# Gated attention and gMLP kernel: the first product of each group is moved to a second PSUM bank by ScalarE and the second product is accumulated onto it there

## The chip, the cores and the metric

The kernel runs on one core of one Trainium2 chip. The metric is the device time of one execution in microseconds (us), from the first to the last instruction of the program with what lies around it. The kernel before took 688.05 us, the median of three runs (686.73, 688.05 and 689.18 us).

## The reference

One input `x` (2048 rows of 1024) goes through two branches, and a gate per row mixes them:

```
gate = sigmoid(sum(x * gate_w))                       # one number per row
# branch A: 32 heads of 32, each row attends to 8 rows at distances 0, 2, ... 14
q, k, v = split(x @ wqkv)
a = softmax(q . k[i - 2w] / sqrt(32)) . v[i - 2w]     # w = 0..7, masked before row 0
a = a @ wo
# branch B: gMLP with F = 3584, Fh = 1792
z  = gelu(x @ w_in);  z1 = z[:, :Fh];  z2 = layernorm(z[:, Fh:])
g  = w_sp @ z2 + b_sp                                 # w_sp is 2048 x 2048: it mixes rows
b  = (z1 * g) @ w_out
out = gate * a + (1 - gate) * b
```

All inputs are bfloat16, and so is the output (2048 by 1024).

## The kernel before, in words

Rows are cut into 16 tiles of 128, which lie in the partitions. TensorE works through five stages, one after the other, in an order that is written out by hand:

1. Projections. `qkv_tile` (matmuls on L603) makes q, k and v for one of eight groups of four heads and one row tile, `z2_tile` (L308) makes z2 in slices of 448 columns. ScalarE copies each finished PSUM bank out (L611, L314). q, k and v are stored to DRAM and come back in a layout in which VectorE can do the sliding attention alone.
2. The z1 stage (L706): 64 tiles of eight matmuls of 448 columns. ScalarE takes each out through a GELU (L708) into one of two staging buffers, which SyncE's queue stores to `z1_d` after every fourth tile (L713). Beside it ScalarE takes sums of squares of z2 (`squares`, L667) and of absolute values of `w_out` (`w_norm`, L539); the latter's pieces are loaded by `load_w_piece` (L536) into two slots by turns. `row_store` (L461 to L470) puts two small transposes into a PSUM bank (L463, L464), which VectorE reads (L465, L466), and stores row scales to DRAM (L470).
3. Mixing, w_sp by z2, 16 groups (`g_group`). A group is a pair of row tiles by half of the columns. A two by two block product is made with seven block products in place of eight (Winograd's scheme of sums); each block product is eight matmuls of 448 columns (L719, the helper `product`). VectorE makes the sums of the operands (L481 to L490). Three banks hold the partial results: `pa` goes on accumulating while ScalarE copies intermediate states of it out (`keep`, L729 and L731, into a ring of five buffers `snaps`), `pd` likewise, and `pb` holds one product alone. VectorE adds a state and a bank, or two states (`vec`, L735), which gives three of the four blocks of g; ScalarE writes the fourth (L762). VectorE then multiplies by z1 (L763). `y_norm` (L559, ScalarE) and `y_scale` (L573, VectorE) rescale the result, and `store_y` (L529) writes it to DRAM from a ring of four buffers, which the groups write by turns.
4. The attention's output by wo (L869), taken out by ScalarE with the gate as scale (L871) into `mix`. It reads `wo` (L439, 2048 KB) and the transposed attention result (L444, 16 transposing DMAs).
5. The last stage, y by w_out, eight groups of seven block products of 512 columns, seven matmuls each (L719 again). `hold` (L880) copies states out with a scale, VectorE adds `mix` to them (L898, L904, L907), and `finish` (L884) scales a bank, adds, and rounds.

The attention itself (L331 to L371) is some 50 VectorE instructions for each group of heads, the longest 4.4 us. It runs beside stages 1 to 3.

The order on each engine is that in which the Python program emits instructions; there is no later scheduler. `Beat` sets it: `beat.now` is a clock that counts TensorE's columns, `beat.vector` one that counts the time that VectorE will be taken for. Each helper of a stage advances the first (`beat.run`) or the second (`beat.on_vector`). Work that is not tied to a matmul waits in a heap with a due time (`beat.at`), and the attention's steps come from a generator, each with a time that it takes. `flush` emits an attention step once its start, by the two clocks, is no more than `LEAD` (3.0 us) ahead of `beat.now`; it stands in VectorE's queue from there on, ahead of whatever the stage emits next. All DMAs of this kernel are issued from SyncE's one queue, in the emitted order; an issue that waits holds back all behind it.

[...] One pool of eight (`psum`, tag "ps") serves all tiles of all stages, so a tile waits until the reader of an earlier tile in the same bank is done.

Of the kernel before, what the change touches and what calls it, by code (L numbers as in the profile page):

```python
# [10 lines left out]
F32 = mybir.dt.float32  # L11
# [4 lines left out]
P = 128  # L16
# [13 lines left out]
ZC = 448  # L30
# [4 lines left out]
W2P = FH + 32  # L35
BEAT = 1.0 / 2360.0
LEAD = 3.0
NU = S // 256
FL = FH // 2
L1_EARLY = 10  # L40
# [20 lines left out]
def kernel(  # L61
# [13 lines left out]
    nc = tc.nc  # L75
# [2 lines left out]

    apool = ctx.enter_context(tc.tile_pool(name="arena", bufs=1))
    sm = ctx.enter_context(tc.tile_pool(name="small", bufs=1))  # L80
    psum = ctx.enter_context(tc.tile_pool(name="psum", bufs=8, space=bass.MemoryType.PSUM))
    dpool = ctx.enter_context(tc.tile_pool(name="dscratch", bufs=1, space=bass.MemoryType.DRAM))

    arena = apool.tile([P, ARENA], BF, name="arena")
# [1 line left out]
    def reg(off, n):  # L86
        return arena[:, off:off + n]
# [10 lines left out]
    warm = reg(R_OFF + 35200, 512)  # L98
    nc.vector.memset(warm, 0.0)

    def warm_up(n):
        pw = psum.tile([P, 512], F32, name="pw", tag="ps")
        for _ in range(n):
            nc.tensor.matmul(pw[:], warm[:, 0:P], warm, start=True, stop=True)

    ident = sm.tile([P, P], BF, name="ident")
    make_identity(nc, ident[:])
# [3 lines left out]
    for jh in range(2):  # L111
        for w in range(W):
            n = min(8, max(0, 14 - 2 * w - 8 * jh))
# [60 lines left out]
    b21, b22 = z2h[:, 8:16, 0:FL], z2h[:, 8:16, FL:FH]  # L174
    t1, t2, t4 = [reg(o, 8 * FL).bitcast(F16).rearrange("p (k f) -> p k f", k=8) for o in (T1_OFF, T2_OFF, T4_OFF)]
# [27 lines left out]
    d11, d12, d21, d22 = [wv[:, h, :, 512 * c:512 * (c + 1)] for h in range(2) for c in range(2)]  # L203
    e1, e2, e4 = [reg(F_OFF + 3584 * r, 3584).bitcast(F16).rearrange("p (k n) -> p k n", n=512) for r in range(3)]
# [29 lines left out]
    class Beat:  # L234
        def __init__(self):
            self.now = 0.0
            self.n = 0
            self.later = []
            self.vector = 0.0
            self.steps = None  # L240
            self.step = None

        def at(self, t, fn):
            heapq.heappush(self.later, (t, self.n, fn))
# [9 lines left out]
        def flush(self, t):  # L254
            while True:
                if self.steps is not None and self.step is None:
                    self.step = next(self.steps, None)
                    if self.step is None:
                        self.steps = None
                due = self.later[0][0] if self.later else 1e12  # L260
                start = max(self.step[0], self.vector) if self.step else 1e12
                if min(due, start - LEAD) > t:
                    return
                if due <= start - LEAD:
                    heapq.heappop(self.later)[2]()
                else:
                    self.vector = start + self.step[1]
                    fn, self.step = self.step[2], None
                    fn()

    beat = Beat()
# [53 lines left out]
    TT = nc.vector.tensor_tensor  # L325
# [209 lines left out]
    def load_w_piece(m):  # L535
        sync.dma_start(w_pieces[m % 2], w_flat[:, 1792 * m:1792 * (m + 1)])  # L536
# [97 lines left out]
    for n in range(L1_EARLY):  # L634
        t = beat.now + 8.0 + 13.0 * n
# [19 lines left out]
    t = beat.now  # L655
# [17 lines left out]
    for i in range(16):  # L673
        for c in range(1 if i > 1 else 2, 4):
            z2_tile(i, c)
        n = L1_EARLY + (i - 3) // 2
# [7 lines left out]
    t = beat.now  # L684
# [3 lines left out]
    beat.at(t + 20.0, row_store)  # L688
    beat.at(t + 22.0, lambda: load_scale(0))
    for m in range(8):  # L690
        beat.at(t + 32.0 + 4.2 * m, lambda m=m: load_w_piece(m))
        beat.at(t + 36.5 + 4.2 * m, lambda m=m: w_norm(m))
    beat.at(t + 70.0, w_total)
    beat.at(t + 91.0, w_power)
# [1 line left out]
    for c in range(4):  # L696
# [3 lines left out]
        for i in range(16):  # L700
# [3 lines left out]
            ps = psum.tile([P, 512], F32, name="ps", tag="ps")  # L704
            for kt in range(KT):
                nc.tensor.matmul(ps[:, 0:ZC], xT[:, kt, i * P:(i + 1) * P], w1[:, kt, :],  # L706
                                 start=(kt == 0), stop=(kt == KT - 1))
# [4 lines left out]
            if i % 4 == 3:  # L712
                sync.dma_start(bass.AP(tensor=z1_d.tensor, offset=z1_d.offset + (i - 3) * P * FH + (2 * (c % 2) + c // 2) * ZC,  # L713
                                       ap=[[FH, P], [P * FH, 4], [1, ZC]]), z1s)
    assert prep["done"]
    def product(ps, w, v, c0, c1, first):
        K = v.shape[1]
        for k in range(K):
            nc.tensor.matmul(ps[:, 0:c1 - c0], w[:, k, :], v[:, k, c0:c1], start=(first and k == 0),  # L719
                             stop=(k == K - 1), skip_group_check=True)  # L720
        beat.run(K * (c1 - c0))
# [3 lines left out]
    def keep(ps, bias):  # L725
        out = snaps[snap[0] % 5]
        snap[0] += 1
        if bias is None:
            nc.scalar.copy(out, ps[:, 0:ZC])  # L729
        else:  # L730
            nc.scalar.activation(out, ps[:, 0:ZC], ACT.Identity, bias=bias)  # L731
        return out

    def vec(out, a, b):
        TT(out, a, b, ALU.add)  # L735
        beat.on_vector(0.65)

    def g_group(n):
        u, f0 = n // 2, n % 2 * ZC
        f1 = f0 + ZC  # L740
        v = pairs[u % 2]
        lo, hi = [bt[:, 2 * u + h:2 * u + h + 1] for h in range(2)]
        g, z = g_ring[n % 4], z1_ring[n % 2]
        now(("z1", n), ("y", u - 2))
        pa, pb, pd = [psum.tile([P, 512], F32, name="ps", tag="ps") for _ in range(3)]
        product(pa, v.a11, b11, f0, f1, True)
        p1 = keep(pa, lo)
        product(pb, v.a12, b21, f0, f1, True)
        vec(g[:, 0, 0], pb[:, 0:ZC], p1)
        product(pa, v.s2, t2, f0, f1, False)  # L750
        u2 = keep(pa, lo)
        product(pd, v.s1, t1, f0, f1, True)
        p5 = keep(pd, None)
        product(pa, v.s3, t3, f0, f1, False)
        u3 = keep(pa, hi)
        if n > 0:
            y_norm(n - 1)
        vec(g[:, 1, 1], p5, u3)
        product(pd, v.s4, b22, f0, f1, False)
        vec(g[:, 0, 1], pd[:, 0:ZC], u2)  # L760
        product(pa, v.a22, t4, f0, f1, False)
        nc.scalar.activation(g[:, 1, 0], pa[:, 0:ZC], ACT.Identity, bias=hi)  # L762
        TT(g, g, z, ALU.mult)  # L763
        beat.on_vector(1.1)
        if n + 2 < 2 * NU:
            soon(("z1", n + 2), lambda: load_z1(n + 2))
# [16 lines left out]
    def y_finish(u):  # L783
        def scaled():
            y_power(u)
            y_scale(u)
            soon(("y", u), lambda: y_done(u))
            if u == NU - 1:
                beat.at(max(beat.now, beat.vector) + 0.6, lambda: load_w_out(1))
# [3 lines left out]
    for n in range(2):  # L793
        load_z1(n)
    for n in range(2 * NU):
        u, fb = n // 2, n % 2
        t = beat.now
        if fb == 0 and u + 1 < NU:
            beat.at(t + 0.5, lambda u=u: load_scale(u + 1))
# [3 lines left out]
        if fb == 0 and u > 0:  # L803
            y_finish(u - 1)
        if fb == 0 and u + 1 < NU:
            for h in range(2):
# [5 lines left out]
        if prep["attended"]:  # L812
            limit = 16 if n >= 2 * NU - 3 else 11
            for m in range(6):
# [3 lines left out]
    t = beat.now  # L818
# [44 lines left out]
    for a in range(16):  # L863
        if a == 12:
            beat.at(beat.now + 0.5, lambda: load_rows_y(2))
        for c in range(2):
            psa = psum.tile([P, 512], F32, name="psa", tag="ps")
            for kt in range(KT):
                nc.tensor.matmul(psa[:], oT[a][:, kt, :], wo_sb[:, kt, 512 * c:512 * (c + 1)],  # L869
                                 start=(kt == 0), stop=(kt == KT - 1))  # L870
# [6 lines left out]
    def hold(ps, scale):  # L877
        out = keeps[kept[0] % 7]
        kept[0] += 1
        nc.scalar.activation(out, ps[:], ACT.Copy, scale=scale)  # L880
        return out

    def finish(out, ps, scale, x):
        nc.vector.scalar_tensor_tensor(out, ps[:], scale, x, ALU.mult, ALU.add)  # L884

    for u in range(NU):
        v = rows[u % 5]
        lo, hi = [omr[:, 2 * u + h:2 * u + h + 1] for h in range(2)]
        m11, m12, m21, m22 = [mix[2 * u + h][:, 512 * c:512 * (c + 1)] for h in range(2) for c in range(2)]
        o11, o12, o21, o22 = [ob_slots[2 * u + h][:, 512 * c:512 * (c + 1)] for h in range(2) for c in range(2)]  # L890
        pa, pb, pd = [psum.tile([P, 512], F32, name="ps", tag="ps") for _ in range(3)]
        if u == 0:
            for n in (3, 4):
                load_rows_y(n)
        product(pa, v.a11, d11, 0, 512, True)
        p1 = hold(pa, lo)
        product(pb, v.a12, d21, 0, 512, True)
        TT(p1, p1, m11, ALU.add)  # L898
        finish(o11, pb, lo, p1)
        product(pa, v.s2, e2, 0, 512, False)  # L900
        u2 = hold(pa, lo)
        product(pd, v.s1, e1, 0, 512, True)
        p5 = hold(pd, hi)
        TT(u2, u2, m12, ALU.add)  # L904
        product(pa, v.s3, e3, 0, 512, False)
        u3 = hold(pa, hi)
        TT(p5, p5, m22, ALU.add)  # L907
        if 0 < u < NU - 1:
            y_sums(u + 1)
        product(pd, v.s4, d22, 0, 512, False)  # L910
        TT(o22, p5, u3, ALU.add)
        finish(o12, pd, lo, u2)
        sync.dma_start(out2[2 * u * P:(2 * u + 1) * P, :], ob_slots[2 * u])
        product(pa, v.a22, e4, 0, 512, False)
        finish(o21, pa, hi, m21)
        if u == NU - 1:
            sync.dma_start(out2[(2 * u + 1) * P:(2 * u + 2) * P, 512:D], o22)
            sync.dma_start(out2[(2 * u + 1) * P:(2 * u + 2) * P, 0:512], o21)
        else:
            sync.dma_start(out2[(2 * u + 1) * P:(2 * u + 2) * P, :], ob_slots[2 * u + 1])  # L920
        if u + 5 < NU:
            load_rows_y(u + 5)
# [30 lines left out]
```

## Time and profile before

| What | Time |
|---|---|
| Time, median of 3 runs | 688.05 us (686.73 to 689.18) |
| Time of the profiled execution | 686.81 us |
| Its span, first to last instruction | 685.0 us |
| TensorE matmul busy | 676.1 us (99%) |
| VectorE busy | 528.8 us (77%) |
| ScalarE busy | 359.9 us (53%) |
| z1 stage (L706) | 270.5 to 369.2 us of the span |
| Mixing (L719, 128x448) | 369.2 to 541.6 us |
| Output of the attention (L869) | 541.6 to 596.8 us |
| Last stage (L719, 128x512) | 596.8 to 681.6 us |

The rows of the profile are read so. In a timeline, a row gives the start in the span, the length, the engine, the source line and the operation; "x42" means that so many instructions in a row were merged; brackets give the idle time of the engine before the row, and what ended it. In a list of waits, a row names who waited for whom, the total, the number of waits and the longest. In a list of groups, the two numbers behind the bar are the group's busy time in us and the mean length of one instruction in ns; then comes the engine's idle time before them. A matmul's length contains its way through the array, and consecutive ones overlap, so a stage's pace is its busy time divided by its matmuls.

### The profile page before, as it was taken

How to read it: one execution, taken by the hardware profiler on the slowest of the kernel's cores; microseconds unless marked ns; L12 is line 12 of the kernel's file. 1: busy time of each engine (PE TensorE's matmuls, PEld its weight loads, DVE VectorE, ACT ScalarE, POOL GpSimd, SP SyncE). 2: the span in 40 equal slices, each digit the busy share in tenths (PEclk: the TensorE clock that was granted, in tenths of full speed). 3: DMA queues.
4: the chain of work that ended last, by engine and by line, in shares of the span. 5: the costliest groups of instructions: out<-in, count | busy, mean ns of one | idle time of the engine just before them, and what ended most of it. 6: DMA issues, size and time to landing. Idle time of an engine off the chain costs nothing. (4 is left out here: it accounts for less than half of the span.)

```text
span 685.0 us, 9426 instructions
## 1 busy us (share of the span) xinstructions
PE 676.1 (99%) x3618; PEld 395.2 (58%) x3618; DVE 528.8 (77%) x578; ACT 359.9 (53%) x674; POOL 13.2 (2%) x23
## 2 busy tenths in 40 slices
PE   9999999999999999999999999999999999999997
PEld 4577788888875555555455454555555444444443
DVE  0009799999999999999999999996996324456755
ACT  4345667565545887848863345445455444422222
POOL 1000000000000000012100000000000000000000
PEclk9999999999999999999999999999999999999999
DMA  8999779998859751446845735756565999755211
GB/s 230 176 229 228 215 183 264 254 256 211 204 128 275 268 179 44 170 108 210 276 152 178 137 76 149 180 132 174 146 163 189 253 233 256 152 112 137 63 62 61
DMA packets 229148, 121.80 MB, mean 178 GB/s; under 512 B 190832, under 2 KB 215664, under 8 KB 229104
## 3 DMA queue, kind: packets, MB, share of 16 engines
q1 hardware_dynamic: 229104, 121.21, 68.1%
q8 instruction: 28, 0.46, 0.3%
q14 instruction: 16, 0.13, 0.1%
HBM read 61.87 MB, written 37.82 MB: 146 GB/s over the span
## 5 line engine op out<-in xcount | busy, mean ns | idle before, releaser
L719 PE MATMUL ps<-arena 128*128 128x448 f16 (+1 forms) x1288 | 255.1, 361 | 2.2 <-ACT arena L729 1.5
L719 PEld LDWEIGHTS <-arena 128*128 128x128 f16 x1288 | 126.0, 98 | 130.9 <-issue 3.2
L603 PE MATMUL ps<-arena 128*128 128x384 bf16 x1024 | 166.7, 326 | 0.8 <-ACT arena L314 0.8
L603 PEld LDWEIGHTS <-arena 128*128 128x128 bf16 x1024 | 141.6, 138 | 25.9 <-issue 1.2
L331 DVE TENSOR_TENSOR arena<-arena 128x8192 bf16<-128x8192 bf16 x16 | 70.7, 4422 | 46.0 <-DMA arena<-k_d 45.8
L706 PE MATMUL ps<-arena 128*128 128x448 bf16 x512 | 97.4, 352 | 1.3 <-ACT arena L708 1.3
L308 PE MATMUL ps<-arena 128*128 128x448 bf16 (+1 forms) x512 | 97.6, 353 | 0.0
L611 ACT CAST arena<-ps 128x384 bf16<-128x384 f32 x112 | 51.6, 482 | 59.5 <-PE ps L603 56.5
L334 DVE TENSOR_TENSOR arena<-arena 128x4096 bf16<-128x4096 bf16 (+1 forms) x64 | 77.6, 1213 | 1.9
L706 PEld LDWEIGHTS <-arena 128*128 128x128 bf16 x512 | 49.9, 98 | 48.0 <-issue 1.6
L308 PEld LDWEIGHTS <-arena 128*128 128x128 bf16 x512 | 50.0, 98 | 46.8 <-ACT arena L295 0.2
L364 DVE TENSOR_TENSOR arena<-arena,att_A 128x8192 bf16<-128x8192 bf16 x16 | 70.7, 4421 | 4.1 <-DMA arena<-v_d 3.9
L731 ACT ACTIVATE arena<-ps,bt 128x448 f32<-128x448 f32 x48 | 30.4, 633 | 68.0 <-PE ps L719 58.3
L869 PE MATMUL psa<-arena 128*128 128x512 bf16 x256 | 55.4, 379 | 0.0
L880 ACT ACTIVATE arena<-ps,omr 128x512 f32<-128x512 f32 x32 | 22.0, 687 | 59.6 <-PE ps L719 59.6
L314 ACT ACTIVATE arena<-ps 128x448 bf16<-128x448 f32 x64 | 34.7, 548 | 31.1 <-PE ps L308 30.4
L708 ACT ACTIVATE arena<-ps 128x448 bf16<-128x448 f32 x64 | 32.5, 558 | 27.8 <-PE ps L706 17.3
L869 PEld LDWEIGHTS <-arena 128*128 128x128 bf16 x256 | 25.0, 98 | 30.2
L871 ACT ACTIVATE arena<-psa,g_s 128x512 f32<-128x512 f32 x32 | 22.0, 686 | 31.4 <-PE psa L869 31.4
L370 DVE TENSOR_TENSOR arena<-arena 128x4096 bf16<-128x4096 bf16 x16 | 36.6, 2287 | 0.3
L451 ACT ACTIVATE arena<-arena 128x2048 bf16<-128x2048 bf16 x16 | 30.8, 1924 | 0.0
L559 ACT ACTIVATE arena<-arena 128x896 bf16<-128x896 bf16 x32 | 30.3, 946 | 0.8 <-DVE arena L763 0.2
(105 smaller groups left out, 447.3 us busy)
## 6 DMA issues: line engine op xcount, KB each, us to landing
arena<-in_B_w_sp_dram SPq DMA_DIRECT2D x16, 512.0 KB, 5.0
arena<-k_d SPq DMA_DIRECT2D x8, 960.0 KB, 6.9
arena<-v_d SPq DMA_DIRECT2D x8, 960.0 KB, 5.7
z_d<-arena SPq DMA_DIRECT2D x16, 448.0 KB, 2.7
arena<-z_d SPq DMA_DIRECT2D x16, 448.0 KB, 3.5
y_d<-arena SPq DMA_DIRECT2D x16, 448.0 KB, 3.1
arena<-in_A_wqkv_dram SPq DMA_DIRECT2D x24, 256.0 KB, 5.4
arena<-in_B_w_in_dram SPq DMA_DIRECT2D x6, 896.0 KB, 7.7
```

What stands on the lines that cost most here:

```text
L308: nc.tensor.matmul(ps[:, 0:N], xT[:, kt, i * P:(i + 1) * P], w2[:, kt, ZC * c:ZC * c + N], start=(kt == 0), stop=(kt == KT - 1))
L314: nc.scalar.activation(z2[:, i, ZC * c:ZC * (c + 1)], ps[:, 0:ZC], ACT.Gelu_apprx_tanh, accum_out=s1[:, 4 * i + c:4 * i + c + 1])
L331: TT(prod.rearrange("p (w j c) -> p w j c", w=W, j=8, c=C), in0, in1, ALU.mult)
L334: return lambda: TT(pv[:, :, 0:half], pv[:, :, 0:half], pv[:, :, half:2 * half], ALU.add)
L364: TT(prod.rearrange("p (w j d h) -> p w j d h", w=W, j=8, d=DH, h=HG), in0, in1, ALU.mult)
L370: return [(4.4, mul), (2.3, lambda: TT(p3[:, 0:4, :], p3[:, 0:4, :], p3[:, 4:8, :], ALU.add)), (1.2, lambda: TT(p3[:, 0:2, :], p3[:, 0:2, ...
L603: nc.tensor.matmul(ps[:, 0:3 * C].rearrange("p (t c) -> p t c", t=3), lhsT, wgt[:, 0:3, kt, :], start=(kt == 0), stop=(kt == KT - 1))
L611: nc.scalar.copy(st[:, j % 4, :], ps[:, 0:3 * C])
L706: nc.tensor.matmul(ps[:, 0:ZC], xT[:, kt, i * P:(i + 1) * P], w1[:, kt, :], start=(kt == 0), stop=(kt == KT - 1))
L708: nc.scalar.activation(z1s[:, i % 4, :], ps[:, 0:ZC], ACT.Gelu_apprx_tanh)
L719: nc.tensor.matmul(ps[:, 0:c1 - c0], w[:, k, :], v[:, k, c0:c1], start=(first and k == 0), stop=(k == K - 1), skip_group_check=True)
L869: nc.tensor.matmul(psa[:], oT[a][:, kt, :], wo_sb[:, kt, 512 * c:512 * (c + 1)], start=(kt == 0), stop=(kt == KT - 1))
```

## The change

It has four parts, and leaves the sums and products of the algorithm as they are, up to the order of additions.

1. The PSUM pool "ps" has six banks, and a new pool `seeded` has two. The warm-up matmuls at the start now write both seeded banks, three each.
2. In `g_group` and in the last stage, ScalarE copies the first product out of `pa` not into SBUF but into a seeded bank (`fork`; in mixing with the bias), and the second product is accumulated onto it there. ScalarE then writes the first block of g from that bank, in place of a VectorE addition. In the last stage `finish` adds `mix` to it directly, and one VectorE addition goes. The second product comes fourth in the order of the seven, no longer second.
3. From the end of the z1 stage on, attention steps are emitted at most `MIX_LEAD` (0.5 us) ahead, no longer 3.0.
4. The pieces of `w_out` are due 2 us earlier, 30 in place of 32.

```
+MIX_LEAD = 0.5
...
-    psum = ctx.enter_context(tc.tile_pool(name="psum", bufs=8, space=bass.MemoryType.PSUM))
+    psum = ctx.enter_context(tc.tile_pool(name="psum", bufs=6, space=bass.MemoryType.PSUM))
+    seeded = ctx.enter_context(tc.tile_pool(name="seeded", bufs=2, space=bass.MemoryType.PSUM))
...
     def warm_up(n):
-        pw = psum.tile([P, 512], F32, name="pw", tag="ps")
-        for _ in range(n):
-            nc.tensor.matmul(pw[:], warm[:, 0:P], warm, start=True, stop=True)
+        for r in range(2):
+            pw = seeded.tile([P, 512], F32, name="pw", tag="sd")
+            for _ in range(n // 2):
+                nc.tensor.matmul(pw[:], warm[:, 0:P], warm, start=True, stop=True)
...
-                if min(due, start - LEAD) > t:
+                if min(due, start - self.lead) > t:
                     return
-                if due <= start - LEAD:
+                if due <= start - self.lead:
...
-        beat.at(t + 32.0 + 4.2 * m, lambda m=m: load_w_piece(m))
+        beat.at(t + 30.0 + 4.2 * m, lambda m=m: load_w_piece(m))
...
     assert prep["done"]
+    beat.lead = MIX_LEAD
...
+    def fork(ps, n, bias):
+        seed = seeded.tile([P, 512], F32, name="seed", tag="sd")
+        if bias is None:
+            nc.scalar.copy(seed[:, 0:n], ps[:, 0:n])
+        else:
+            nc.scalar.activation(seed[:, 0:n], ps[:, 0:n], ACT.Identity, bias=bias)
+        return seed
...
-        pa, pb, pd = [psum.tile([P, 512], F32, name="ps", tag="ps") for _ in range(3)]
+        pa, pd = [psum.tile([P, 512], F32, name="ps", tag="ps") for _ in range(2)]
         product(pa, v.a11, b11, f0, f1, True)
-        p1 = keep(pa, lo)
-        product(pb, v.a12, b21, f0, f1, True)
-        vec(g[:, 0, 0], pb[:, 0:ZC], p1)
+        pb = fork(pa, ZC, lo)
+        product(pd, v.s1, t1, f0, f1, True)
+        p5 = keep(pd, None)
         product(pa, v.s2, t2, f0, f1, False)
         u2 = keep(pa, lo)
-        product(pd, v.s1, t1, f0, f1, True)
-        p5 = keep(pd, None)
+        product(pb, v.a12, b21, f0, f1, False)
+        nc.scalar.copy(g[:, 0, 0], pb[:, 0:ZC])
         product(pa, v.s3, t3, f0, f1, False)
...
         product(pa, v.a11, d11, 0, 512, True)
-        p1 = hold(pa, lo)
-        product(pb, v.a12, d21, 0, 512, True)
-        TT(p1, p1, m11, ALU.add)
-        finish(o11, pb, lo, p1)
+        pb = fork(pa, 512, None)
+        product(pd, v.s1, e1, 0, 512, True)
+        p5 = hold(pd, hi)
         product(pa, v.s2, e2, 0, 512, False)
         u2 = hold(pa, lo)
-        product(pd, v.s1, e1, 0, 512, True)
-        p5 = hold(pd, hi)
+        product(pb, v.a12, d21, 0, 512, False)
+        finish(o11, pb, lo, m11)
```

## Prediction before the result

> **What bounds the kernel.** I read the page's busy rows and slices, then TensorE's timeline for its holes, then who ends each hole: ScalarE's and VectorE's timelines there, and SyncE's for the DMAs.
>
> ```profile
> span 685.0 us, 9426 instructions
> ...
> PE 676.1 (99%) x3618; PEld 395.2 (58%) x3618; DVE 528.8 (77%) x578; ACT 359.9 (53%) x674; POOL 13.2 (2%) x23
> ...
> PEclk9999999999999999999999999999999999999999
> ```
> TensorE is the bound, at full granted clock throughout. Only its holes can be won; anything that delays it is lost one for one.
>
> ```profile
> 1.19 2.74 PE L104 MATMUL pw<-arena 128*128 128x512 bf16 x6 [1.19 <-DVE arena L99]
> ...
> 291.80 0.22 PE L463 MATMUL pt<-ident,rs_n 128*16 128x128 bf16 x1
> ...
> 292.06 48.60 PE L706 MATMUL ps<-arena 128*128 128x448 bf16 x256
> 341.98 21.35 PE L706 MATMUL ps<-arena 128*128 128x448 bf16 x112 [1.31 <-ACT arena L708]
> ...
> 389.09 30.65 PE L719 MATMUL ps<-arena 128*128 128x448 f16 x160 [1.52 <-ACT arena L729]
> 420.25 121.47 PE L719 MATMUL ps<-arena 128*128 128x448 f16 x640 [0.51 <-ACT arena L731]
> 541.56 55.42 PE L869 MATMUL psa<-arena 128*128 128x512 bf16 x256
> 596.81 84.77 PE L719 MATMUL ps<-arena 128*128 128x512 f16 x392
> ```
> Three holes matter: 1.31 us in the z1 stage, 1.52 and 0.51 in mixing. A z1 tile takes (48.60 - 0.16) / 32 = 1.514 us (0.16 is the last matmul's way through the array), and a product of mixing the same, eight matmuls of 448 columns. The last two stages have none.
>
> ```profile
> 382.90 4.43 DVE L331 TENSOR_TENSOR arena<-arena 128x8192 bf16<-128x8192 bf16 x1
> 387.24 0.62 DVE L735 TENSOR_TENSOR arena<-arena 128x448 bf16<-128x448 f32 x1
> ```
> ```profile
> 388.51 0.53 ACT L729 COPY arena<-ps 128x448 f32<-128x448 f32 x1 [3.30 <-DVE arena L735]
> ```
> The 1.52: an addition stood behind a 4.43 us attention step, its `snaps` buffer stayed taken, ScalarE could not copy, TensorE waited.
>
> ```profile
> 300.25 0.15 DVE L466 TENSOR_TENSOR bt<-pt,rs 128x16 f32<-128x16 bf16 x1
> ```
> ```profile
> 338.28 1.70 ACT L539 ACTIVATE arena<-arena 128x1792 bf16<-128x1792 bf16 x1 [0.79 <-DMA arena<-in_B_w_out_dram]
> ...
> 341.39 1.42 ACT L708 ACTIVATE arena<-ps 128x448 bf16<-128x448 f32 x3
> ```
> `row_store`'s bank, written at 291.80, is not read until 300.25: VectorE was at attention. And at 341 ScalarE, late behind `w_norm`, released the bank that TensorE waited for.
>
> ```profile
> 521.73 0.57 SPq L385 DMA_DIRECT2D o_d<-arena  x1
> 525.83 0.37 SPq L439 DMA_DIRECT2D arena<-wop_d  x1
> 526.30 0.52 SPq L523 DMA_DIRECT2D arena<-z_d  x1
> 526.88 9.58 SPq L444 DMA_TRANSPOSE arena<-o_d  x2
> 536.57 1.04 SPq L529 DMA_DIRECT2D y_d<-arena  x2
> 537.66 12.06 SPq L444 DMA_TRANSPOSE arena<-o_d  x8
> ```
> Behind the 2 MB of `wo`, two transposes held SyncE for 9.58 us and the y stores with them.
>
> **The change part by part.**
>
> *Six banks instead of eight in the z1 stage.* Before, the seventh tile after `row_store` takes over its bank: it starts at 292.06 + 6 x 1.514 = 301.14, after the read's end at 300.40. In the changed program's order the fifth does, ready at 298.12. VectorE's queue up to there is unchanged, so TensorE waits 300.44 - 298.12 = 2.3 us. At 341 the same eviction now releases a tile two earlier, which TensorE reaches at 340.67 - 3.03 + 2.3 = 339.9: a wait of 2.0 if the eviction stays put. Together 4.3 against 1.3: +3.0, two tiles. Against that the earlier pieces of `w_out`: ScalarE waited 1.47 and 0.79 us for them (page group L539: 3.2 in all). At most 2.3 comes back, at least nothing. I take 0.4, near the low end: SyncE waited 4.5 us for `w_norm` to free a slot (L536 on L539), which an earlier due time doesn't change. Part: **+2.6** (0.7 to 3.0). In the projections ScalarE's lag is covered: their holes are 0 with eight banks, and I find no reader there as late as L466. If one were, the price is up to 3.0, but it would be paid out of the same two tiles at 300.
>
> *Seeding in mixing.* Per group VectorE loses one addition (L735, 618 ns; 16 of them 9.9 us), ScalarE gains one copy (L729's 532 ns; 8.5 us), and `keep` becomes `fork` at a like size (L731, 633 ns). ScalarE waited 68.0 us before its 48 L731 and has room. TensorE's columns are the same. ScalarE's write into PSUM is in no row: if it cost nothing that would gain nothing, and it may last up to 1.5 us before `pa`'s next product, one product later, would wait. I take 633 ns, no effect. The first read of the seed comes two products later. The ring of five `snaps` now takes three states a group, not four, and with 0.5 us of lead the additions stand ahead of the attention step that they followed at 387. So both holes go: **-2.0** (1.52 + 0.51; ends 0 and -2.2, L719's whole idle time). The cover is ScalarE's room; without it each of 16 copies would cost up to 0.53, 8.5 us in all.
>
> *What is late next: the first block of g, now on ScalarE.* It overwrites a buffer of the ring of four, so it waits for that buffer's y store, and all ScalarE evictions queue behind it. The attention ends sooner: VectorE drops about 12 additions before its end (7.4 us) and waits of 12.5 us (L735 on L731), so the last `o_d` store goes from 521.7 to about 500 (498 to 502, an estimate from these). In the changed order it and `wo` stand ahead of the last pair's two row transposes (512 KB each), two z1 loads and five oT transposes, and only then come the y stores that group 14 needs. `wo` at 500 + 4.1 = 504.1; before, 10.7 us from `wo` to the y stores with two transposes of 256 KB; now nine such portions, seven more at 12.06 / 8 = 1.51: 21.3 us, so 525.4, and landed 2.6 to 3.1 later: 528.0 to 528.5. Group 14 starts at 369.2 + 2.6 + 14 x 10.6 = 520.2; its fourth product ends at 526.3, and TensorE feels it if ScalarE starts this copy after 528.1 (two products more, less 0.53 + 0.63 of copies). **+0.4** (0 to 3). The rows of the last pair land near 518 with VectorE's sums done near 520.5, needed at 521.7: hidden, by 1 us.
>
> *The last stage.* 8 x 693 ns of VectorE go (L898), `fork` replaces `hold`; TensorE had no hole: 0. Warm-up in two banks: the same six matmuls, 0. The end (L884, then the store) is unchanged.
>
> Sum: +2.6 - 2.0 + 0.4 = +1.0. The profiled execution took 686.81 us (span 685.0), 1.24 under the median; 687.8 there, **689.0** against the median.
>
> [...]
>
> **The rivals.**
>
> *Slower: the store queue decides.* If `wo` and the transposes hold SyncE longer than reckoned, or the attention ends at 502, every us past 528.1 is lost. The 5.15 us that the first oT transpose took behind `wo` speaks for it; that before's y stores at 536.57 stalled nothing speaks against, but there VectorE wrote g and the ring hid it. At 2 us more: 691.0; it passes 0.3% from about 1.1 us on. Chance 0.20.
>
> *Faster: the z1 stage gives back.* If the pieces land early, the wait near 341 goes: +0.7 - 2.0 = -1.3, 686.7. Ordinary executions run 1.24 longer than the profiled one; if that is mixing's waits, they go too: 685.5. Chance 0.13.
>
> *The seeding removes nothing.* If the additions still stand behind attention steps, mixing keeps its 2.0: 691.0. Against it: the order shows them ahead. Chance 0.07.
>
> *The clock drops in a longer hole.* The start shows the slow rate: 2.74 / 6 = 0.46 us a matmul of 512 columns against 55.42 / 256 = 0.216, full by 5.89. One such drop of 4.7 us costs half, 2.4: 691.4. Against it: after holes of 1.31 and 1.52 the clock row stays at 9, and mine are 2.3 and 1.6. Chance 0.05. [...]
>
> **How the numbers follow.** Forecast, within 1.3 us of 689.0: 0.55. A measurement of this kernel tells about 0.3% from no change, 2.1 us (its runs spread over 2.5). Slower than 690.1: the queue 0.16, no removal 0.06, the clock 0.05, the forecast's upper end 0.03: 0.30. Faster than 686.0: 0.10, from the z1 rival and its median. The rest, 0.60, is within. Range 686.6 to 692.0: the low end takes in the z1 rival as seen from the profiled execution, the high end a queue that costs 3.
>
> **What would show it.** Right: one hole of about 2.3 us near 298 that VectorE L466 ends, one of 1 to 2 near 341, none from 372 to 520, the `o_d` store near 500, at most a short hole near 528. Wrong: no hole at 298; holes in mixing ended by ScalarE's copy of a state; a hole over 1.5 us near 520 to 530; a clock row below 9; a fork much over 0.7 us.

## The result, and the profile after

The changed kernel takes 689.96 us, the median of seven runs (688.79 to 691.16); the kernel before took 687.46 beside it (seven runs, 686.05 to 689.18). The ratio is 1.0038 with a 95% interval of 1.0023 to 1.0054: slower by 2.5 us. The prediction was 689.0 within 686.6 to 692.0. The time lies inside, but the mechanism was only half right: one of the rivals, at a chance of 0.05, is part of it. The profiled execution took 689.91 us, 3.1 more than the one of before.

The page, first its busy rows and its clock row:

```profile
span 688.1 us, 9397 instructions
...
PE 677.1 (98%) x3618; PEld 395.6 (57%) x3618; DVE 514.2 (75%) x554; ACT 367.0 (53%) x690; POOL 13.1 (2%) x23
...
PEclk9999999999999999999999999999999999999999
```

VectorE lost 14.6 us of work and ScalarE gained 7.1, as the change says; TensorE is the bound before and after. The clock row still shows 9 throughout, and that is deceptive: a slice is 17.2 us, and 3.41 us at half clock in it give 0.90. TensorE's timeline has the holes and the starts of the stages:

```profile
292.50 6.23 PE L710 MATMUL ps<-arena 128*128 128x448 bf16 x32
300.96 39.51 PE L710 MATMUL ps<-arena 128*128 128x448 bf16 x208 [2.23 <-DVE bt L470]
343.17 26.06 PE L710 MATMUL ps<-arena 128*128 128x448 bf16 x128 [2.70 <-ACT arena L712]
...
375.14 4.70 PE L725 MATMUL ps<-arena 128*128 128x448 f16 x24
...
544.63 55.42 PE L883 MATMUL psa<-arena 128*128 128x512 bf16 x256
599.88 4.70 PE L725 MATMUL ps<-arena 128*128 128x512 f16 x21
```

Against the rows of before: the z1 stage starts 0.44 us later (TensorE waits 0.42 us for the load of `x` at 4.46; no part of the change, as the kernel with eight banks below starts the stage at 270.49), mixing starts at 375.14 in place of 369.24, and lasts 169.49 us in place of 172.32; the two stages behind it last as long as before. So the z1 stage lost 5.46 us and mixing gave back 2.83. Of the 5.46, the two holes are 2.23 + 2.70 - 1.31 = 3.62, with 0.16 more for one more break of TensorE's row. (In the kernel before a row of 256 matmuls takes 48.60 us and one of 112 takes 21.35: 0.189 us for each matmul, and 0.16 for each row.) The rest is found only when the stretch behind the second hole is cut finely. The windows view shows, for each stretch, its length, the busy time of each engine with its instructions, and then the granted clock, DMA share and GB/s:

```profile
core 0: us, PE busy (x) PEld busy (x) DVE busy (x) ACT busy (x) POOL busy (x), PEclk, DMA share, GB/s
298.94:302.36 3.42, 1.40 (x8) 0.76 (x8) 3.35 (x8) 0.37 (x1) 0.00 (x0) 1.00 0.07 12
302.36:305.77 3.41, 3.41 (x20) 1.77 (x19) 3.38 (x2) 2.65 (x4) 0.00 (x0) 1.00 0.95 265
339.91:343.32 3.41, 0.71 (x4) 0.29 (x3) 3.38 (x5) 3.38 (x5) 0.00 (x0) 1.00 1.03 348
343.32:346.73 3.41, 3.41 (x10) 1.37 (x9) 3.38 (x5) 3.41 (x7) 0.00 (x0) 0.50 0.62 227
```

For 3.41 us after the second hole the clock was 0.50: ten matmuls where 20 go at full clock. That costs half the stretch, 1.7 us, and 3.62 + 0.16 + 1.7 is the 5.46. After the first hole, of 2.23 us, the clock stayed at 1.00.

Why the second hole is 2.70 and not 2.0 stands in ScalarE's timeline:

```profile
336.41 0.63 ACT L353 ACTIVATE att_L<-att_L 128x512 f32<-128x512 f32 x1
339.47 1.70 ACT L543 ACTIVATE arena<-arena 128x1792 bf16<-128x1792 bf16 x1 [2.43 <-DMA arena<-in_B_w_out_dram]
341.07 0.19 ACT L543 ACTIVATION_READ_ACCUMULATOR arena<-arena 128x1 f32 x1
341.28 1.28 ACT L712 ACT_TABLE_LOAD   x1
342.57 1.42 ACT L712 ACTIVATE arena<-ps 128x448 bf16<-128x448 f32 x3
```

`w_norm` (L543 here) stands between the softmax's exponential (L353) and the evictions (L712). It waited 2.43 us for its piece of `w_out`, where before it was 0.79, and the evictions came at 342.57, 1.18 us later than before. The earlier due time took away the earlier wait of 1.47, and the next piece was late instead.

### The profile page after: what moved, and what is told of

The parts are those of the page before. It is cut to its first block, busy times and chain, and to the rows that moved or that the text cites. A ratio compares the mean times of both kernels' runs of the same rounds, so it can differ in the third digit from the quotient of the medians.

```text
span 688.1 us, 9397 instructions
## 1 busy us (share of the span) xinstructions
PE 677.1 (98%) x3618; PEld 395.6 (57%) x3618; DVE 514.2 (75%) x554; ACT 367.0 (53%) x690; POOL 13.1 (2%) x23
## 4 chain that ended last, share of the span: by engine, by line
PE 84%; DVE 6%; ACT 3%; DMA 3%; SPq 2%; issue 1%; ACTq 0%; DVEq 0%
PE ps L725 32%; PE ps L607 24%; PE ps L312 10%; PE psa L883 8%; PE seed L725 5%; PE ps L710 5%; DMA z_d<-arena 2%; SPq L592 1%; DVE arena L368 1%; ACT arena L671 1%; ACT arena L712 1%; ACT arena L543 1%; DVE arena L338 1%; DVE arena L512 1%; DMA arena<-in_A_wqkv_dram 1%; DVE arena L335 1%
## 5 line engine op out<-in xcount | busy, mean ns | idle before, releaser
L725 PE MATMUL ps<-arena 128*128 128x448 f16 (+1 forms) x1104 | 222.0, 361 | 0.0
L335 DVE TENSOR_TENSOR arena<-arena 128x8192 bf16<-128x8192 bf16 x16 | 70.7, 4420 | 46.9 <-DMA arena<-k_d 46.7
L710 PE MATMUL ps<-arena 128*128 128x448 bf16 x512 | 99.2, 356 | 4.9 <-ACT arena L712 2.7
L712 ACT ACTIVATE arena<-ps 128x448 bf16<-128x448 f32 x64 | 33.4, 560 | 33.7 <-PE ps L710 25.7
L898 DVE SCALAR_TENSOR_TENSOR arena<-seed,omr,arena 128x512 bf16<-128x512 f32 x8 | 6.0, 751 | 56.2 <-PE seed L725 56.2
L725 PE MATMUL seed<-arena 128*128 128x448 f16 (+1 forms) x184 | 40.2, 361 | 0.0
L737 ACT ACTIVATE arena<-ps,bt 128x448 f32<-128x448 f32 x32 | 20.3, 633 | 29.5 <-PE ps L725 27.5
L894 ACT ACTIVATE arena<-ps,omr 128x512 f32<-128x512 f32 x24 | 16.5, 687 | 32.8 <-PE ps L725 32.8
```

The costliest lines, as they stand in the source:

```text
L335: TT(prod.rearrange("p (w j c) -> p w j c", w=W, j=8, c=C), in0, in1, ALU.mult)
L712: nc.scalar.activation(z1s[:, i % 4, :], ps[:, 0:ZC], ACT.Gelu_apprx_tanh)
```

## The experiments

Each ratio is to the kernel before, measured on the same chip; line numbers differ by a few between the kernels.

### Six banks alone

The kernel before with the smaller pool and nothing else.

```
-    psum = ctx.enter_context(tc.tile_pool(name="psum", bufs=8, space=bass.MemoryType.PSUM))
+    psum = ctx.enter_context(tc.tile_pool(name="psum", bufs=6, space=bass.MemoryType.PSUM))
```

> The kernel before with a PSUM pool of six banks in place of eight, and nothing else. Theory (two banks fewer cost the z1 stage): a hole of about 2.2 us near 298 ended by VectorE's L466, and one of 2 to 2.8 near 341; the z1 stage ends some 3.0 us later than before, 4.7 if the clock falls for 3.4 us after a hole of over 2 us, as it did in the changed kernel. Since TensorE then reaches mixing later against VectorE's attention, the holes of mixing may move; with them as before the time is about 690.5 to 692 us (3.0 to 4.7 over before), without them 688 to 690. Rival (the loss comes from the new order of copies and loads, not from the banks): no new hole in the z1 stage, the time within 1 us of before.

690.39 us, ratio 1.0048 (1.0035 to 1.0061). TensorE's timeline (the profiled execution was the longest, 694.11 us; the five others took 690.05 to 690.69, so they lost less than it shows):

```profile
301.88 39.52 PE L706 MATMUL ps<-arena 128*128 128x448 bf16 x208 [2.26 <-DVE bt L466]
346.12 27.08 PE L706 MATMUL ps<-arena 128*128 128x448 bf16 x128 [4.72 <-ACT arena L708]
```

The pool alone makes both holes. Here, with the pieces due at 32, ScalarE waited 2.54 and 1.88 us for them, the second hole is 4.72 us, and half clock lasts 6.83 us behind it. Mixing had no hole although nothing was changed there: TensorE starts it 9.9 us later than before, at 379.12, and VectorE starts its first attention step there (L331) only 4.3 us later (376.69 for 372.43), so it is further on with the attention by then.

### The short lead alone

The kernel before with `MIX_LEAD` 0.5 from the end of the z1 stage; eight banks, no seeding.

```
+MIX_LEAD = 0.5
...
+            self.lead = LEAD
...
-                if min(due, start - LEAD) > t:
+                if min(due, start - self.lead) > t:
...
-                if due <= start - LEAD:
+                if due <= start - self.lead:
...
     assert prep["done"]
+    beat.lead = MIX_LEAD
```

> The kernel before with the attention emitted at most 0.5 us ahead from mixing on, eight banks and no seeding. Theory A (the shorter lead is what clears mixing): no hole from 372 to 540, the z1 stage as before with its one hole of 1.3 near 341; 2.0 to 2.8 us faster than before, about 685.0. Theory B (the seeding is what clears mixing, with one addition less on VectorE): the two holes of 1.5 and 0.5 us stay, or others take their place; within 0.7 us of before, 687 to 688.

684.54 us, ratio 0.9968 (0.9957 to 0.9978), without a hole in mixing and with one of 1.53 us near 341:

```profile
342.52 21.35 PE L708 MATMUL ps<-arena 128*128 128x448 bf16 x112 [1.53 <-ACT arena L710]
369.79 169.66 PE L722 MATMUL ps<-arena 128*128 128x448 f16 x896
```

One number clears mixing; no second bank is needed for it.

### Eight banks for the z1 stage of the changed kernel

Every fourth z1 tile takes a seeded bank, so that the stage works in eight again; some tiles of the attention's output take one too, which writes both seeded banks over their full width ahead of the last stage.

```
-            ps = psum.tile([P, 512], F32, name="ps", tag="ps")
+            if (16 * c + i) % 4 == 3:
+                ps = seeded.tile([P, 512], F32, name="ps", tag="sd")
+            else:
+                ps = psum.tile([P, 512], F32, name="ps", tag="ps")
...
-            psa = psum.tile([P, 512], F32, name="psa", tag="ps")
+            if a == 1:
+                psa = seeded.tile([P, 512], F32, name="psa", tag="sd")
+            else:
+                psa = psum.tile([P, 512], F32, name="psa", tag="ps")
```

> The changed kernel, but every fourth tile of the z1 stage takes one of the two seeded banks, which lie idle there, so that the stage runs through eight banks again; the tiles of row block 1 in the attention's output stage use the seeded banks too. Theory (the banks are the loss, mixing is a gain): no hole near 298, one of 0.9 to 1.5 us near 341, no fall of the clock, mixing without holes; about 684.7 us, 2.5 to 3.0 under before and 5 under the changed kernel. Rival (the loss comes from the pieces of w_out, which now stand ahead of a z1 store): the hole near 341 stays at 2 us or more and the time is 687 or more.

684.97 us, ratio 0.9975 (0.9964 to 0.9986).

```profile
292.04 48.60 PE L713 MATMUL ps<-arena 128*128 128x448 bf16 x256
342.39 21.35 PE L713 MATMUL ps<-arena 128*128 128x448 bf16 x112 [1.75 <-ACT arena L715]
```

The hole near 298 is gone, the one near 341 is 1.75 us (a little more than the theory's 0.9 to 1.5), and the granted clock of the profiled execution is 1.000. So with eight banks the whole loss is gone, and what remains of the change is the gain of the short lead: 684.54 without the seeding, 684.97 with it.

### The pieces due at 32 again

The changed kernel with its fourth part undone.

```
-        beat.at(t + 30.0 + 4.2 * m, lambda m=m: load_w_piece(m))
+        beat.at(t + 32.0 + 4.2 * m, lambda m=m: load_w_piece(m))
```

> The changed kernel with the pieces of w_out due at 32 again. If the earlier pieces help, as I took 0.4 us for it, this is 0.4 us slower than the changed kernel, the hole near 341 some 3 us. If they cost, because a piece now stands ahead of the z1 store that ScalarE waits for near 305, ScalarE's wait there ends about 0.6 us sooner and the hole near 341 is about 2 us: 0.5 us faster, or 2.2 if the clock then stays up. The hole near 298 is 2.2 us in both cases.

690.81 us, ratio 1.0054 (1.0034 to 1.0075); the second hole is 4.04 us rather than 2.70, with one stretch of 3.41 us at half clock as in the changed kernel. So the earlier pieces were worth 1.3 us of this hole; by the two ratios it is 1.1 us, which the intervals do not tell from nothing.

### The seeding without the short lead

The kernel with eight banks in the z1 stage, and the lead of 3.0 again.

```
-MIX_LEAD = 0.5
+MIX_LEAD = 3.0
```

> The changed kernel with every fourth z1 tile in a seeded bank, so that eight banks serve the z1 stage, and with the attention issued 3.0 us ahead in mixing as before: what is left of the change is the seeding. Theory (the lead clears mixing, the seeding does little there): holes of about 1.5 us in the mixing stage, ended by a ScalarE copy of a state that waits for VectorE, and 686.5 to 688.0 beside a kernel before of 687, ratio 0.998 to 1.002. Rival (the seeding clears mixing by itself, one state fewer in the ring): no hole in mixing, ratio 0.9975 as the kernel with the eight banks and the short lead had it. Second rival (ScalarE's wait for the y store, hidden in the changed kernel, comes through since the attention and with it the y store end later): a hole of 1 to 3 us near 528, ratio 1.001 to 1.004.

691.95 us, ratio 1.0073 (1.0061 to 1.0085): worse than each of the three cases said. First TensorE's timeline in mixing, then ScalarE's:

```profile
412.83 1.69 PE L728 MATMUL ps<-arena 128*128 128x448 f16 x8 [0.29 <-DVE arena L485]
414.69 3.20 PE L728 MATMUL ps<-arena 128*128 128x448 f16 x16 [0.17 <-DVE arena L489]
...
508.51 6.21 PE L728 MATMUL ps<-arena 128*128 128x448 f16 x32 [1.33 <-ACT arena L740]
...
532.88 7.90 PE L728 MATMUL ps<-arena 128*128 128x448 f16 x32 [3.03 <-ACT arena L740]
```

```profile
507.39 0.53 ACT L770 CAST arena<-seed 128x448 bf16<-128x448 f32 x1 [4.08 <-DMA y_d<-arena]
...
531.76 0.53 ACT L770 CAST arena<-seed 128x448 bf16<-128x448 f32 x1 [5.78 <-DMA y_d<-arena]
```

The wait on which the prediction put its slower rival (ScalarE writes the first block of g into a buffer whose y store is not done) comes through twice. The attention ends sooner: its last store is issued at 488.99, against 496.81 with the same banks and the short lead (502.30 in the changed kernel, which is later in mixing). So `wo`, issued at 494.30, and the transposes that follow it meet the y stores: one pair, issued at 496.70 between them, is not done until 507, and the next stands behind the transposes and is issued at 527.21. Against the kernel with the same banks and the short lead, the spans (690.1 and 682.6) differ by 7.5 us: 4.8 us of holes, 0.6 for four more breaks of TensorE's row at 0.16, 1.7 for a stretch of 3.41 us at a clock of 0.50 behind the hole of 3.03, and 0.3 by which mixing started later. So the seeding brings a new wait, and the short lead, by holding the attention back, hides it. The two holes of before, at 387 and 420, are gone here too: up to 412 mixing runs without one. The seeding does clear those two by itself, and puts 4.8 us of others in their place.

### row_store in a bank of its own

In the changed kernel, `row_store`'s transposes go to a seeded bank. Two matmuls write both seeded banks over their full width before mixing, which costs 0.4 us (374.72 to 375.15).

```
-        pt = psum.tile([P, 4, P], BF, name="pt", tag="ps")
+        pt = seeded.tile([P, 4, P], BF, name="pt", tag="sd")
...
     assert prep["done"]
+    for _ in range(2):
+        pw = seeded.tile([P, 512], F32, name="pw", tag="sd")
+        nc.tensor.matmul(pw[:], xT[:, 0, 0:P], xT_flat[:, 0:512], start=True, stop=True)
```

> The changed kernel with row_store's transposes in a seeded bank, which the z1 tiles do not use; six banks for the tiles as in the changed kernel. Theory (what is lost is two tiles of run-ahead in all, whichever late reader shows it): the hole near 298 goes, and TensorE comes 2.2 us earlier to the late ScalarE eviction near 341, so that the holes from 300 to 345 come to 4.5 to 5.5 us in all, and the time is within 1 us of the changed kernel's, ratio 1.003 to 1.006 to the kernel before. Rival (row_store's bank is a loss of its own): 2.7 us of hole near 341 is all that is left, 2.2 us less than the changed kernel, ratio 1.000 to 1.001.

689.82 us, ratio 1.0047 (1.0033 to 1.0061), no better than the changed kernel.

```profile
312.11 27.40 PE L710 MATMUL ps<-arena 128*128 128x448 bf16 x144 [1.20 <-ACT arena L712]
343.02 25.78 PE L710 MATMUL ps<-arena 128*128 128x448 bf16 x128 [3.52 <-ACT arena L712]
```

The hole near 298 is gone and 4.72 us are there all the same, 1.20 at 311 and 3.52 near 341 (changed kernel: 4.93). So the loss is one of run-ahead, whichever late reader collects it.

### The pieces further apart

The changed kernel, with 4.8 us for each piece and each sum.

```
-        beat.at(t + 30.0 + 4.2 * m, lambda m=m: load_w_piece(m))
-        beat.at(t + 36.5 + 4.2 * m, lambda m=m: w_norm(m))
-    beat.at(t + 70.0, w_total)
+        beat.at(t + 30.0 + 4.8 * m, lambda m=m: load_w_piece(m))
+        beat.at(t + 36.5 + 4.8 * m, lambda m=m: w_norm(m))
+    beat.at(t + 75.0, w_total)
```

> The changed kernel with the eight w_out pieces and their sums of magnitudes 4.8 us apart rather than 4.2, so that ScalarE has 4.8 us for each and its evictions stand less far behind near 341. Theory (the eviction near 341 was late because ScalarE was behind with the sums and waiting for pieces): the hole near 298 stays 2.2 us, the one near 341 is under 1.7 us, the granted clock stays at full, and the time is 2.5 to 3.5 us under the changed kernel's, ratio 0.998 to 1.001 to the kernel before. Rival (the two loads of ScalarE's function table around the softmax's exponential make it late by themselves): a hole of 2.3 to 2.8 us near 341 remains, and the ratio is 1.002 to 1.005, with or without the stretch at half clock.

686.07 us, ratio 1.0001 (0.9984 to 1.0018); two of the eleven executions took longer than the rest, 688.98 and 691.80. TensorE's timeline, then ScalarE's:

```profile
301.14 39.51 PE L710 MATMUL ps<-arena 128*128 128x448 bf16 x208 [2.14 <-DVE bt L470]
341.33 24.37 PE L710 MATMUL ps<-arena 128*128 128x448 bf16 x128 [0.68 <-ACT arena L712]
```

```profile
338.79 0.63 ACT L353 ACTIVATE att_L<-att_L 128x512 f32<-128x512 f32 x1
339.44 1.28 ACT L712 ACT_TABLE_LOAD   x1
340.73 0.98 ACT L712 ACTIVATE arena<-ps 128x448 bf16<-128x448 f32 x2
```

No sum stands between the exponential and the evictions any more. The hole near 341 falls from 2.70 to 0.68, the granted clock of the profiled execution is 1.000, and with that the loss against the kernel before is gone, although the stage has six banks and the hole near 298 is there. The price of the six banks is not gone: with eight banks in the z1 stage and all else the same (below, "The same with the seeding") the ratio is 0.9955, 3.2 us less. The gains of the lead and of the spacing cover it.

### The short lead and the wider spacing, without the seeding

The edit against the kernel with the short lead alone:

```
-        beat.at(t + 32.0 + 4.2 * m, lambda m=m: load_w_piece(m))
-        beat.at(t + 36.5 + 4.2 * m, lambda m=m: w_norm(m))
-    beat.at(t + 70.0, w_total)
+        beat.at(t + 30.0 + 4.8 * m, lambda m=m: load_w_piece(m))
+        beat.at(t + 36.5 + 4.8 * m, lambda m=m: w_norm(m))
+    beat.at(t + 75.0, w_total)
```

> The kernel before with the short lead in mixing, and with the eight w_out pieces first due at 30 and 4.8 us apart, as their sums: no seeding, eight banks. Theory (the same ScalarE lag makes the 1.53 us hole near 341 of the kernel with the short lead alone): that hole falls under 0.6 us, and the time is 683.0 to 684.0, ratio 0.994 to 0.996. Rival (the table loads alone make it): the hole stays at 1.2 to 1.6 us, 684.3 to 684.8, ratio 0.9965.

682.42 us, ratio 0.9938 (0.9925 to 0.9951): 4.3 us faster than the kernel before, and faster than both kernels of this case; it is 0.6 us under the range that the theory gave. The z1 stage and mixing run without any hole:

```profile
291.78 69.79 PE L708 MATMUL ps<-arena 128*128 128x448 bf16 x368
...
367.48 169.66 PE L722 MATMUL ps<-arena 128*128 128x448 f16 x896
```

### The same with the seeding

The changed kernel with eight banks in the z1 stage (its edit as above) and the spacing of 4.8 us.

> The changed kernel with eight banks in the z1 stage and the w_out pieces 4.8 us apart: the change with what it loses in the z1 stage taken out. Theory (TensorE has no hole left that the seeding could fill): the same time as the kernel without the seeding with the short lead and the spaced pieces, ratio 0.993 to 0.995 to the kernel before. Rival (the seeding takes something off TensorE's way by itself): under 0.992.

684.02 us, ratio 0.9955 (0.9941 to 0.9969). That is 0.0005 above what the theory gave, and above the rival's 0.992. Near 390 TensorE waits 0.91 and 0.17 us for VectorE's sums of the operands (L485, L489). VectorE's timeline shows why: an attention step of 4.43 us (L335) starts at 383.45, ahead of the sums at 388.79. In the kernel without the seeding the same step starts at 389.72, behind the sums at 384.27. With one addition less in VectorE's queue the step comes up sooner; that this is what moved it is argued, not tested. The seeding puts nothing on top of the short lead.

### Holes made on purpose

The kernel with the short lead and the spacing, and in the last stage sixteen places where TensorE waits for a chain of VectorE operations of no use (three, four and five maxima in the three kernels; the third takes them over 464 columns, not 448).

```
+    def stall():
+        px = psum.tile([P, 512], F32, name="px", tag="ps")
+        nc.tensor.matmul(px[:, 0:1], ident[:], ident[:, 0:1], start=True, stop=True)
+        nc.vector.tensor_copy(L[:, 0:1], px[:, 0:1])
+        for _ in range(3):
+            TT(L[:, 0:448], L[:, 0:448], L[:, 0:448], ALU.max)
+        nc.vector.tensor_copy(att_A[:, 0:1], L[:, 0:1])
+        nc.tensor.matmul(px[:, 1:2], ident[:], att_A[:, 0:1], start=True, stop=True)
...
         product(pa, v.a11, d11, 0, 512, True)
+        stall()
...
         product(pd, v.s1, e1, 0, 512, True)
+        stall()
```

> The kernel with the short lead and the spaced pieces, and sixteen holes made on purpose in the last stage, two a group of products: TensorE waits each time for a chain of VectorE operations, here about 2.0 to 2.3 us long. Theory (the clock looks at stretches of about 3.4 us, and halves for the next such stretch when some two thirds to four fifths of one were idle): none of the sixteen is followed by half clock, or one or two at the most; the kernel is longer by the holes alone, 32 to 37 us. Rival (a hole's length alone decides, from a bound between 2.3 and 2.7 us on): none.

> The same with chains that make holes of about 2.6 to 2.8 us. Theory (stretches of 3.4 us): where the hole lies against the stretch decides, so that 4 to 9 of the sixteen are followed by 3.41 us at half clock and the others by none, at 1.7 us each, 7 to 15 us beyond the holes. Rival (length alone, from a bound between 2.3 and 2.7 us on): all sixteen, 27 us beyond the holes. [...]

> The same with chains that make holes of about 3.2 to 3.4 us. Theory (stretches of 3.4 us): more of them, 8 to 13 of sixteen. Rival (length alone from 2.3 to 2.7 us on): all sixteen. [...]

The holes came out longer than meant, 2.45, 3.11 and 3.85 us, each alike within 0.01. Single executions took 740.49, 762.33 and 774.13 us. Behind ten of sixteen holes of 2.45 the clock fell, behind all sixteen of 3.11, and behind fifteen of sixteen of 3.85: the longest holes were not the surest, so that length alone does not decide. The forecast numbers were missed, too. The half clock lasted 3.41 us or twice that, 6.83, and within one kernel it began only at times that are multiples of 3.41 us apart (595.62, 605.85, 616.09 and on in the kernel with the holes of 2.45 us). Cut at those times, the windows of the kernel with the holes of 2.45 us read:

```profile
592.21:595.62 3.41, 1.12 (x7) 0.49 (x5) 2.08 (x5) 1.02 (x2) 0.00 (x0) 1.00 1.09 214
595.62:599.03 3.41, 3.25 (x9) 1.19 (x9) 0.74 (x3) 0.00 (x0) 0.00 (x0) 0.50 0.24 54
602.44:605.85 3.41, 1.32 (x8) 0.61 (x8) 3.13 (x6) 0.36 (x1) 0.00 (x0) 1.00 0.00 0
605.85:609.26 3.41, 3.41 (x10) 1.21 (x9) 0.69 (x1) 0.69 (x1) 0.00 (x0) 0.50 0.02 5
619.51:622.92 3.41, 1.79 (x10) 0.78 (x8) 1.45 (x4) 1.37 (x2) 0.00 (x0) 1.00 0.00 0
622.92:626.33 3.41, 2.58 (x13) 1.19 (x13) 3.38 (x7) 0.69 (x1) 0.00 (x0) 1.00 0.00 0
```

The windows in which TensorE was busy for 1.12 and 1.32 us were followed by one at half clock; a hole of the same 2.45 us that is split over two windows, busy for 1.79 and 2.58, was followed by none. In the kernel with the holes of 3.85 us it is the first hole that escapes, cut nearly in the middle:

```profile
592.72:596.13 3.41, 1.45 (x8) 0.67 (x7) 1.79 (x4) 1.34 (x2) 0.00 (x0) 1.00 1.00 205
596.13:599.55 3.42, 1.54 (x9) 0.70 (x9) 2.32 (x5) 0.00 (x0) 0.00 (x0) 1.00 0.29 64
599.55:602.96 3.41, 3.19 (x16) 1.47 (x15) 0.91 (x2) 0.88 (x2) 0.00 (x0) 1.00 0.00 0
```

The theory's kind was right as far as these traces show it (stretches of 3.41 us, at fixed times in each of them) and its bound wrong: not two thirds to four fifths idle, but some 60%. A window with 1.32 us busy, 61% idle, was followed by half clock, and one with 1.40 us, 59% idle, was not: the second is the changed kernel's own window at 298.94. Cut in the same way, no window at full clock breaks this in the other traces with half clock behind a hole (six banks alone, the pieces due at 32, `row_store` apart, the seeding without the short lead).

## Why the prediction was right or wrong

**Six banks, +2.6.** The hole near 298 was right in size (2.23 for 2.3), in place and in its reader, and the argument of the two tiles stood the test of `row_store` in a bank of its own. Two terms were mis-sized. "If the eviction stays put": it came 1.18 us later; TensorE itself was 0.6 later there than reckoned, and 2.0 became 2.70. The earlier pieces bring more than the 0.4 taken (1.3 of hole with the pieces back at 32), but off a larger loss: with six banks and the pieces at 32 the hole near 341 is 4.0 to 4.7 us, not 2.0, as ScalarE's sums then wait twice for their pieces. The part came to 5.46, 3.8 of holes and 1.7 of clock, above the high end of 3.0. One row was misread without effect: the projections are not free of holes with eight banks. TensorE waits 0.75 us for ScalarE at 22.08 in the kernel before, and 0.88 us for a DMA there in the changed one.

**The clock, a rival at 0.05.** This is the step that failed. "After holes of 1.31 and 1.52 the clock row stays at 9, and mine are 2.3 and 1.6" took the length of a hole for the measure, and 2.3 us for short enough, where no hole of the kernel before is longer than 1.52. The row that it went by cannot show such a drop either: it reads 9 in the changed kernel too, with 3.41 us at 0.50. By the two values above, 1.32 and 1.40 us busy, a hole from about 2.05 us on could drop the clock if it lies in one window (an estimate: 3.41 less their middle, 1.36; the shortest that did was 2.45), so that the forecast hole of 2.3 us was already within reach. The price, 2.4, was too high: it took the 4.7 us at the start for the length of a drop, but the stretch behind the hole of 2.70 lasted 3.41 us and cost 1.7. In the kernels with holes made on purpose a drop lasted 3.41 or 6.83 us, and holes of 2.45 us brought one in ten cases of sixteen.

**Mixing, -2.0.** All holes went, and the stage is 2.83 us shorter: 2.18 us of idle time; of the other 0.65 no run shows the cause (two breaks of TensorE's row, at 0.16 each, would be half of it). The size was near; the cause named, seeding and lead together ("the ring of five `snaps` now takes three states a group, not four, and with 0.5 us of lead ..."), is more than it takes. The lead alone clears mixing. The seeding alone clears these two holes but is 5 us slower than the kernel before. Even six banks alone, by making TensorE late, leave none. In the changed kernel all three are there (TensorE starts mixing 5.9 us later than before), so which of them did it cannot be told apart.

**The first block of g on ScalarE, +0.4.** The y stores were issued at 527.54, the last attention store at 502.30, both about 2 us later than reckoned, as mixing was 3.3 us later than reckoned. ScalarE waited 1.98 us, and TensorE not at all: the copy started at 530.80, half a microsecond before TensorE would have felt it by the prediction's own reckoning (mixing from 375.14, fourteen groups of 10.6, four products of 1.5, and 1.8 more). So 0, and a near thing; the seeding with the long lead shows the rival's price, with a hole of 3.03 us.

**The write into PSUM.** 609 ns against 633 into SBUF, as the groups show:

```profile
L737 ACT ACTIVATE arena<-ps,bt 128x448 f32<-128x448 f32 x32 | 20.3, 633 | 29.5 <-PE ps L725 27.5 <-DVE arena L490 1.0 <-DVE arena L485 1.0
...
L749 ACT ACTIVATE seed<-ps,bt 128x448 f32<-128x448 f32 x16 | 9.7, 609 | 14.1 <-PE ps L725 14.1
```

The write into the seeded bank is shorter by 24 ns of 633, which hide beside TensorE; the z1 stage, 5.46 us longer with two banks fewer, is what decided the time. **The last stage, 0:** right, 88.2 us from its start to the end of the span in both.

**The whole.** 689.0 was 1 us short of the median, and that near by luck. The change was reckoned at +1.0; the medians of seven give +2.5, and the profiled executions +3.1. Half of the error was covered by the 1.24 us that were added because a median of three executions lay so far over the profiled one. Later medians of the kernel before, of 9 to 19 executions beside the experiments, are 686.73 to 686.92, close to its profiled 686.81, and the changed kernel's median is close to its profiled 689.91. Between the profiled executions, where 687.8 was reckoned and 689.91 came, the errors are +2.9 in the z1 stage, -0.8 in mixing, -0.4 at the y stores, and the start's 0.44, which is not the change's. By the prediction's bound of 0.3%, the outcome is slower, to which 0.30 was given, with 0.60 on no change.

## What to carry to other kernels

Before banks are taken from a pool that is shared by all stages, look for the stage that needs their run-ahead: two banks cost here some two tiles and the clock stretch behind them, wherever a late reader stood, and moving one reader only handed the wait to the next. What helped was to make the late reader less late. When a change has several parts, price each alone: here the smallest edit held all of the gain, and another part had a wait that only that edit hid. And reckon with a half-clock stretch behind a hole in a chain of matmuls: here it cost 1.7 us behind the hole of 2.70, and came behind ten of sixteen holes of 2.45 us, while none followed the holes of up to 2.26 us.

## What the runs showed of the hardware that was not expected

- In the traces with half clock behind a hole, cut into windows of 3.41 us at the times where the half clock began, TensorE's clock was 0.50 for the next window behind every window at full clock in which TensorE was busy for 1.32 us or less (39%), and 1.00 behind every one with 1.40 us or more (41%). The windows do not start with the work, so holes of the same 2.45 us brought half clock, 1.7 us for a window of it, in ten places and none in six. From half clock it came back after a window with 0.78 us idle (the pieces due at 32), and not after windows with 1.3 (six banks alone) and 1.6 us idle (the holes of 3.85 us); where that bound lies was not measured.
- Such a stretch does not show in the page's clock row: 3.41 us at 0.50 in a slice of 17 us still read 9.
- A hole can also vanish because TensorE is late elsewhere: mixing's holes went in the kernel with six banks alone, where nothing in mixing was changed (TensorE started it 9.9 us later and ran it as one row of 169.88 us).
